# Full-row score matmuls in place of 64-row pairs, and projections issued between retention steps, in a kernel of three blocks

## The chip, the cores and the metric

The kernel runs on one core of a Trainium2 chip. The time is the device time of one execution in microseconds, the median of three runs. A profile is one more execution, taken by the hardware profiler; all rows in this document come from such profiles.

## What is computed

Three blocks follow each other, for 8 batches of 576 positions and 512 channels:

```python
scores = scale * np.matmul(q, k.transpose(0, 1, 3, 2))        # 8 heads of 64
ret = scores * Dmat[None, :, :, :]                            # causal, gamma ** (i - j)
x = np.matmul(ret, v)                                         # retention
...
for e in range(E):                                            # 4 experts of 64
    q = x @ wq[e]; k = x @ wk[e]; v = x @ wv[e]
    scores = np.where(causal, -1000000000.0, scale * (q @ k.transpose(0, 2, 1)))
    a = softmax(scores)
    out += gate_e * (a @ v @ wo[e])                           # top 2 of 4 experts
...
theta = x @ w_theta
y = w_tok_r @ (x * cos(theta)) + w_tok_i @ (x * sin(theta))
u = x + y
out = u + np.maximum(u @ w_ch, 0.0)
```

## The kernel before, in words

**Numbers.** Products that need more precision than one pass gives are made from a high and a low part of each operand: `split` writes the high part on ScalarE and the difference on VectorE, and `mm3` issues three matmuls (high by high, high by low, low by high).

**Stages.** The first half of the span handles retention and the experts' attention, batch by batch; the second half (`z_tile`, `mix`, `channel`) mixes over positions and channels. The change is in the first half.

**Retention** (`ret_fill`) goes over a batch in five chunks of 128 rows (the last has 64). Step c issues the scores of chunk c (`ret_scores`, L125, masked on VectorE at L130 and L133) and the output of chunk c-1 (`ret_out`: state L146, products L153 and L157). The output becomes rows of x: xt on VectorE (L164), its high part xh on ScalarE (L166), its low part xl on POOL (L167). Then the loads of a later chunk are issued on SP's queue, and v is scaled on POOL (L111).

**Projections** read x: `proj_v` for one chunk of rows (12 matmuls of 260 columns), `proj_qk` for half the rows (g) of K (t = 1) or Q (t = 0) of a pair p of experts (12 matmuls of 288 columns). Q goes into `U` [128, 2, S]: for expert s of the pair, one half of the partitions holds the high part and the other half the low part. The high part of K goes into `KN`, and after its second half four DMAs copy it into `KK`, expert by expert, to both halves of the partitions. The low part goes into `KL`.

**Attention** runs in units (batch, pair, row tile m of 5), 80 in all. `at_scores` multiplies for each expert s of the pair all 128 rows of U with KK (high and low of Q times high of K, L272), and then the 64 rows with the high part of Q with KL (L275); VectorE masks the result and takes the minimum (L278), ScalarE makes exp and its sum (L283). `at_norm` scales P (L292 to L299). `at_trans` transposes P on TensorE (L324) and copies it to PT on VectorE for s = 0 and ScalarE for s = 1 (L329, L331). `at_out` multiplies PT with V (L343). It runs when a group of row tiles, (0), (1, 2) or (3, 4), is complete.

**Order.** The loop over units interleaves a unit with *filler*: the second pair's projections of this batch, then everything that the next batch needs first. Each filler has a planned cost; `fill(lim, k)` issues fillers until the planned costs reach `lim`. A unit's planned cost stands in `COST`. A scheduler underneath moves instructions of one engine by the times that it expects itself, so that the built order differs from the written one in places.

**Buffers.** PSUM has four buffers "a" for scores, transposes and value products, and three "w" for retention and projections. `KN` has one buffer, `U`, `KK` and `KL` two.

Of the kernel before, what the change touches and what calls it, by code (L numbers as in the profile page):

```python
# [44 lines left out]
FO = 0.5  # L45
# [8 lines left out]
def tile_kernel(ctx: ExitStack, tc: tile.TileContext, qk, kv, w1, wo, wot, wd, cst, out):  # L54
# [129 lines left out]
    def proj_qk(b, p, t, g):  # L184
        xh, xl = XT[b]
        if (b, p) not in QKP:
            QKP[b, p] = (att.tile([128, 2, S], F32R, name="U", bufs=2), att.tile([128, 2, S], F32R, name="KK", bufs=2),
                         att.tile([128, S], F32R, name="KL", bufs=2), att.tile([128, S], F32R, name="KN", bufs=1))
        U, KK, KL, KN = QKP[b, p]
# [5 lines left out]
        if t:  # L195
            split(KN[:, sl], KL[:, sl], ps)
            if g:
                for s in range(2):
                    for o in range(2):
                        nc.sync.dma_start(KK[o * 64:o * 64 + 64, s, :].bitcast(F32),  # L200
                                          KN[s * 64:s * 64 + 64, :].bitcast(F32))
            return
# [53 lines left out]


    PB, PTB, OB = {}, {}, {}

    def at_scores(u):  # L260
        b, p, m = u
        U, KK, KL, _ = QKP[b, p]
# [6 lines left out]
        for i, (j0, j1) in enumerate(parts):  # L269
            ps = [ps1.tile([128, j1 - j0], F32, name="a", bufs=AB, padded_shape=[128, 512]) for _ in range(2)]  # L270
            for s in range(2):
                nc.tensor.matmul(ps[s][:R], U[:, s, rs], KK[:, s, j0:j1], start=True, stop=False)  # L272
            for s in range(2):
                hs = slice(s * 64, s * 64 + 64)
                nc.tensor.matmul(ps[s][:R], U[hs, s, rs], KL[hs, j0:j1], start=False, stop=True)  # L275
            o = 512 - C * m
            for s in range(2):
                MARK["dve"] = nc.vector.tensor_tensor_reduce(  # L278
                    Ps[s][:R, j0:j1], ps[s][:R], cm[:R, o + j0:o + j1], 1.0, st[:R, 0, s:s + 1] if i else 3.0e38,
                    OP.add, OP.min, st[:R, i, s:s + 1])  # L280
# [231 lines left out]
    COST = [0.7, 1.1, 1.6, 2.2, 2.2]  # L512
    fillers = []
    for b in range(B):
        f1 = qk_fill(b, 1)
        f2 = ret_fill(b + 1) + v_fill(b + 1) + qk_fill(b + 1, 0) if b + 1 < B else []
# [18 lines left out]
    for t in range(nu + 1):  # L535
# [5 lines left out]
        if t < nu:  # L541
            at_scores(units[t])
            done += COST[units[t][2]]
        if t >= 1:
            at_trans(units[t - 1])
        goal = tot * (k + 1) / 10 if t < nu else 1e9
        fill(goal - FO, k)
# [4 lines left out]
        if t < nu:  # L552
            at_norm(units[t])
        fill(goal, k)
# [236 lines left out]
```

## Time and profile before

| | |
|---|---|
| median of 3 runs | 989.08 us (987.85 to 990.68) |
| profiled execution | 989.46 us, span 987.7 us |
| TensorE busy (PE) | 958.8 us, 97% of the span, 8090 matmuls |
| VectorE (DVE) | 683.4 us, 69% |
| ScalarE (ACT) | 487.1 us, 49% |
| GpSimd (POOL) | 226.7 us, 23% |
| granted TensorE clock | 0.991 of full on average |

PE is TensorE's matmuls, PEld its weight loads; the two overlap. Matmul records overlap too, because a matmul's record lasts until its last column has left the array; how fast TensorE goes is read from the starts of the records. L272 is line 272 of the kernel. A timeline merges equal instructions that follow each other into one row with a count. "Idle" is time in which an engine did nothing before an instruction, and behind an arrow stands what ended it; "issue" means that the profile shows nothing that it waited for.

### The profile page before, as it was taken

To read this page: it belongs to the slowest core of one execution; us is meant where nothing else is said; L and a number is where in the kernel's file an instruction comes from. 1 tells how busy PE (TensorE), PEld (TensorE's weight loads), DVE (VectorE), ACT (ScalarE), POOL (GpSimd) and SP (SyncE) were. 2 spreads that over 40 slices of the span, in tenths; PEclk is the share of its full clock that TensorE was granted. 3 is DMA by queue.
4 is the path that set the end of the run, shared out by engine and by line. 5 is a ranking of instruction groups with operands and counts; after the bars stand their busy time and mean duration, and the time that the engine had idled before them with its cause. 6 is when DMAs were issued, how large, how long until landed. Compare 5 with 4: busy or idle time off the path is not lost.

```text
span 987.7 us, 21586 instructions
## 1 busy us (share of the span) xinstructions
PE 958.8 (97%) x8090; PEld 848.1 (86%) x8090; DVE 683.4 (69%) x2099; ACT 487.1 (49%) x1278; POOL 226.7 (23%) x278
## 2 busy tenths in 40 slices
PE   6999999999999999999999999999999999999998
PEld 6988878778787877777767899999999999999998
DVE  5498887888978779687576783485655746486533
ACT  2366656656666565566567652344333432344320
POOL 4334262452624525332000001020200102020110
PEclk9999999999999999999999999999999999999999
DMA  9755563654635636354631301010001001010001
GB/s 267 199 166 155 154 194 89 195 172 124 212 111 171 194 106 204 98 163 132 243 127 37 121 2 48 14 60 25 36 13 37 37 1 49 1 38 12 25 26 48
DMA packets 64185, 101.45 MB, mean 103 GB/s; under 512 B 15184, under 2 KB 37072, under 8 KB 64080
## 3 DMA queue, kind: packets, MB, share of 16 engines
q1 hardware_dynamic: 63936, 99.79, 33.1%
q8 instruction: 64, 1.05, 0.4%
q0 software_dynamic: 144, 0.28, 0.1%
q14 instruction: 41, 0.34, 0.1%
HBM read 67.22 MB, written 23.66 MB: 92 GB/s over the span
## 4 chain that ended last, share of the span: by engine, by line
PE 83%; DVE 10%; DMA 3%; issue 1%; ACT 1%; SPq 1%; POOL 1%; ACTq 0%; POOLq 0%
PE acc L658 24%; PE w L87 12%; PE w L88 11%; PE w L89 11%; PE a L343 4%; PE a L324 4%; PE a L272 3%; PE a L275 2%; PE w L125 2%; PE w L157 2%; PE w L153 2%; PE acc L648 2%; DMA kv<-kv 2%; DVE P L278 2%; DVE sm L130 1%
## 5 line engine op out<-in xcount | busy, mean ns | idle before, releaser
L658 PE MATMUL acc<-TK,zh 128*128 128x256 f32 (+1 forms) x1024 | 183.8, 302 | 0.0
L658 PEld LDWEIGHTS acc<-TK,zh 128*128 128x128 f32 x1024 | 152.4, 190 | 0.7 <-DVE ul L93 0.2
L684 POOL TENSOR_TENSOR o<-o,ul 128x576 f32<-128x576 f32 x28 | 41.9, 1500 | 435.2 <-DVE o L679 435.2
L283 ACT ACTIVATE P<-P,st 128x128 f32<-128x128 f32 (+4 forms) x160 | 95.8, 599 | 69.4 <-DVE st L278 68.6
L658 PE MATMUL acc<-TK,zl 128*128 128x256 f32 (+1 forms) x512 | 110.0, 297 | 0.0
L278 DVE CUSTOM_DVE_ANT_0 P<-a,cm 128x128 f32<-128x128 f32 (+4 forms) x160 | 72.8, 476 | 26.9 <-PE a L275 26.4
L658 PEld LDWEIGHTS acc<-TK,zl 128*128 128x128 f32 x512 | 86.2, 189 | 0.1
L602 ACT ACTIVATE cs<-cs 128x512 f32<-128x512 f32 x72 | 45.2, 630 | 80.3 <-DVE cs L600 76.7
L92 ACT ACTIVATE zh<-cs 128x512 fp32r<-128x512 f32 x64 | 40.2, 630 | 81.3 <-PE acc L658 67.0
L87 PE MATMUL w<-xh,WH 128*128 128x288 f32 x256 | 79.9, 312 | 0.0
L93 DVE TENSOR_TENSOR zl<-cs,zh 128x512 fp32r<-128x512 f32 x64 | 45.0, 707 | 50.4 <-ACT zh L92 49.4
L88 PE MATMUL w<-xl,WH 128*128 128x288 f32 x256 | 76.3, 298 | 0.0
L324 PE MATMUL a<-ident,P 128*128 128x128 f32 (+2 forms) x480 | 65.2, 265 | 11.1 <-DVE P L297 5.2
L87 PE MATMUL w<-uh,CH 128*128 128x256 f32 (+1 forms) x256 | 75.8, 296 | 0.0
L89 PE MATMUL w<-uh,CH 128*128 128x256 f32 (+1 forms) x256 | 75.8, 296 | 0.0
L88 PE MATMUL w<-ul,CH 128*128 128x256 f32 (+1 forms) x256 | 75.8, 296 | 0.0
L89 PE MATMUL w<-xh,WL 128*128 128x288 f32 x256 | 75.6, 295 | 0.0
L604 DVE SCALAR_TENSOR_TENSOR cs<-cs,x 128x512 f32<-128x512 f32 x72 | 55.4, 775 | 24.6 <-ACT cs L602 24.5
L125 PE MATMUL w<-qz,kt 128*64 128x256 f32 (+1 forms) x576 | 61.8, 334 | 7.7 <-DMA kt<-qk 5.1
L167 POOL TENSOR_TENSOR xl<-xt,xh 128x512 fp32r<-128x512 f32 (+1 forms) x40 | 50.7, 1269 | 78.8 <-ACT xh L166 78.8
L324 PEld LDWEIGHTS a<-ident,P 128*128 128x128 f32 (+2 forms) x480 | 45.7, 138 | 26.1 <-DVE P L297 7.4
L93 DVE TENSOR_TENSOR ul<-acc,uh 128x256 fp32r<-128x256 f32 x64 | 25.7, 450 | 59.3 <-ACT uh L92 59.1
(141 smaller groups left out, 2484.7 us busy)
## 6 DMA issues: line engine op xcount, KB each, us to landing
kv<-kv SPq DMA_DIRECT2D x40, 512.0 KB, 4.8
KK<-KN SPq DMA_DIRECT2D x64, 144.0 KB, 2.5
raw<-wd SPq DMA_DIRECT2D x43, 192.0 KB, 2.8
qz<-qk SPq DMA_DIRECT2D x64, 128.0 KB, 4.1
kt<-qk SPq DMA_DIRECT2D x32, 256.0 KB, 3.7
out<-o SPq DMA_DIRECT2D x28, 288.0 KB, 2.1
td<-hl SPq DMA_DIRECT2D x27, 192.0 KB, 2.5
TK<-td SPq DMA_DIRECT2D x9, 576.0 KB, 8.0
```

What stands on the lines that cost most here:

```text
L87: nc.tensor.matmul(ps, ah, bh, start=first, stop=False)
L88: nc.tensor.matmul(ps, ah, bl, start=False, stop=False)
L89: nc.tensor.matmul(ps, al, bh, start=False, stop=last)
L93: nc.vector.tensor_sub(l, src, h)
L125: nc.tensor.matmul(ps[e][g, i, :, j * 64:R], t[:, hp, j * 64:j * 64 + 64], qz[:, :, hp, j * 64:R], start=True, stop=True, skip_group_check ...
L167: nc.gpsimd.tensor_sub(xl[:, :, cs], xt, xh[:, :, cs])
L278: MARK["dve"] = nc.vector.tensor_tensor_reduce(Ps[s][:R, j0:j1], ps[s][:R], cm[:R, o + j0:o + j1], 1.0, st[:R, 0, s:s + 1] if i else 3.0e3 ...
L283: MARK["act"] = nc.scalar.activation(Ps[s][:R, :n], Ps[s][:R, :n], AF.Exp, bias=st[:R, last, s:s + 1], scale=-1.0, accum_out=st[:R, 2, s:s ...
L324: nc.tensor.transpose(tp[:w, j, :], Ps[s][:R, j * C:j * C + w], ident[:R, :R])
L602: nc.scalar.activation(cs, cs, AF.Sin)
L604: nc.vector.scalar_tensor_tensor(z, cs, -1.0, x2[:, None, ds].to_broadcast([128, 2, 256]), op0=OP.mult, op1=OP.mult)
L658: nc.tensor.matmul(acc[d][j], A[:, dc], TK[:, kt, W, t0:t1], start=q == 0 and n == 0, stop=q == 8 and n == 2)
```

## The change

It does four things. The low part of K goes into the same tile as the high part (`KN` and `KK` get one more dimension, `KL` goes), so that the DMAs copy both to both halves of the partitions; `at_scores` then issues for each expert two matmuls with all 128 rows, so that the low part of Q times the low part of K is now computed too. `next_fill` puts V, K and Q projections of the next batch between its retention steps, each after the step that writes the rows that it reads, where they all stood behind the last step before. The unit's order changes: scores, 45% of the filler, normalising of this unit, transposes of the unit before, the rest of the filler, value product. And the planned costs of units are a little larger.

```diff
--- before.py
+++ after.py
@@ -42,7 +42,7 @@
 WARM = 50
 AB = 4
 WB = 3
-FO = 0.5
+FO = 0.45
 NDVE = (0,)
 JR = 82
 EARLY = 9
@@ -184,21 +184,21 @@
     def proj_qk(b, p, t, g):
         xh, xl = XT[b]
         if (b, p) not in QKP:
-            QKP[b, p] = (att.tile([128, 2, S], F32R, name="U", bufs=2), att.tile([128, 2, S], F32R, name="KK", bufs=2),
-                         att.tile([128, S], F32R, name="KL", bufs=2), att.tile([128, S], F32R, name="KN", bufs=1))
-        U, KK, KL, KN = QKP[b, p]
+            QKP[b, p] = (att.tile([128, 2, S], F32R, name="U", bufs=2), att.tile([128, 2, 2, S], F32R, name="KK", bufs=2),
+                         att.tile([128, 2, S], F32R, name="KN", bufs=1))
+        U, KK, KN = QKP[b, p]
         w0 = (2 * p + t) * 128
         sl = slice(g * HS, g * HS + HS)
         ps = ps1.tile([128, HS], F32, name="w", bufs=WB, padded_shape=[128, 512])
         for kt in range(4):
             mm3(ps, WH[:, kt, w0:w0 + 128], WL[:, kt, w0:w0 + 128], xh[:, kt, sl], xl[:, kt, sl], kt == 0, kt == 3)
         if t:
-            split(KN[:, sl], KL[:, sl], ps)
+            split(KN[:, 0, sl], KN[:, 1, sl], ps)
             if g:
                 for s in range(2):
                     for o in range(2):
-                        nc.sync.dma_start(KK[o * 64:o * 64 + 64, s, :].bitcast(F32),
-                                          KN[s * 64:s * 64 + 64, :].bitcast(F32))
+                        nc.sync.dma_start(KK[o * 64:o * 64 + 64, s, :, :].bitcast(F32),
+                                          KN[s * 64:s * 64 + 64, :, :].bitcast(F32))
             return
         for s in range(2):
             i, o = slice(s * 64, s * 64 + 64), slice(64 - s * 64, 128 - s * 64)
@@ -254,12 +254,17 @@
     def v_fill(b):
         return [(1.31, lambda c=c: proj_v(b, c)) for c in range(NCH)] + [(0.0, lambda: gate(b))]
 
+    def next_fill(b):
+
+        r, v, q = ret_fill(b), v_fill(b), qk_fill(b, 0)
+        return [*r[:3], v[0], r[3], v[1], q[0], r[4], v[2], q[2], r[5], v[3], q[1], v[4], v[5], q[3]]
+
 
     PB, PTB, OB = {}, {}, {}
 
     def at_scores(u):
         b, p, m = u
-        U, KK, KL, _ = QKP[b, p]
+        U, KK, _ = QKP[b, p]
         R = ROWS[m]
         n = min(C * (m + 1), S)
         rs = slice(m * C, m * C + R)
@@ -269,10 +274,8 @@
         for i, (j0, j1) in enumerate(parts):
             ps = [ps1.tile([128, j1 - j0], F32, name="a", bufs=AB, padded_shape=[128, 512]) for _ in range(2)]
             for s in range(2):
-                nc.tensor.matmul(ps[s][:R], U[:, s, rs], KK[:, s, j0:j1], start=True, stop=False)
-            for s in range(2):
-                hs = slice(s * 64, s * 64 + 64)
-                nc.tensor.matmul(ps[s][:R], U[hs, s, rs], KL[hs, j0:j1], start=False, stop=True)
+                for x in range(2):
+                    nc.tensor.matmul(ps[s][:R], U[:, s, rs], KK[:, s, x, j0:j1], start=x == 0, stop=x == 1)
             o = 512 - C * m
             for s in range(2):
                 MARK["dve"] = nc.vector.tensor_tensor_reduce(
@@ -509,11 +512,11 @@
         X2[g, i], NR[g, i] = x2, nr
 
     units = [(b, p, m) for b in range(B) for p in range(2) for m in range(NCH)]
-    COST = [0.7, 1.1, 1.6, 2.2, 2.2]
+    COST = [0.9, 1.2, 1.7, 2.2, 2.4]
     fillers = []
     for b in range(B):
         f1 = qk_fill(b, 1)
-        f2 = ret_fill(b + 1) + v_fill(b + 1) + qk_fill(b + 1, 0) if b + 1 < B else []
+        f2 = next_fill(b + 1) if b + 1 < B else []
         fillers.append(f1 + f2)
 
     nu = len(units)
@@ -541,17 +544,17 @@
         if t < nu:
             at_scores(units[t])
             done += COST[units[t][2]]
+        goal = tot * (k + 1) / 10 if t < nu else 1e9
+        fill(done + FO * max(goal - done, 0.0), k)
+        if t < nu:
+            at_norm(units[t])
         if t >= 1:
             at_trans(units[t - 1])
-        goal = tot * (k + 1) / 10 if t < nu else 1e9
-        fill(goal - FO, k)
+        fill(goal, k)
         if t >= 1:
             ub, up, um = units[t - 1]
             if GROUPS[GRP[um]][-1] == um:
                 at_out(ub, up, GRP[um])
-        if t < nu:
-            at_norm(units[t])
-        fill(goal, k)
 
 
         for _ in range(0 if t < 2 else t * JR // 100 - (t - 1) * JR // 100):
```

Behind the change, lines of the kernel are 3 to 6 higher: the scores are L278, the mask L281, exp L286, the normalising L295 to L302, the transposes L327, the copies L332 and L334, the value product L346.

How the built order changes shows at three places, all in the middle of the first half. First on TensorE, scores of row tile 2 while projections are the filler (L272 and L275, after L278: scores; L324, after L327: transposes; L343, after L346: value product; L87 to L89: the three matmuls of a projection, of V where `WH` stands before `xh`, of K or Q the other way round). Before:

```order
L87 MATMUL w<-WH,xh 128x260
L88 MATMUL w<-WL,xh 128x260
L89 MATMUL w<-WH,xl 128x260
L272 MATMUL a<-KK,U 128x384 x2
L275 MATMUL a<-KL,U 128x384 x2
L324 MATMUL a<-ident,P 128x128 x4
L87 MATMUL w<-WH,xh 128x260
```

After:

```order
L89 MATMUL w<-WH,xl 128x260
L346 MATMUL a<-PT,V 64x128 x2
L278 MATMUL a<-KK,U 128x384 x4
L87 MATMUL w<-xh,WH 128x288
L88 MATMUL w<-xl,WH 128x288
L89 MATMUL w<-xh,WL 128x288
...
L89 MATMUL w<-xh,WL 128x288
L327 MATMUL a<-ident,P 128x128 x4
L153 MATMUL w<-qz_110,S_107 64x64 x8
```

The 64-row pair is gone, four equal matmuls stand in its place, and a whole projection stands between them and the transposes.

Second on TensorE, a retention step that ends with L157, and scores of row tile 0. Before:

```order
L272 MATMUL a<-KK,U 128x128 x2
L275 MATMUL a<-KL,U 128x128 x2
L125 MATMUL w<-qz_110,kt 64x2x64 x3
L324 MATMUL a<-ident,P 128x64 x4
L324 MATMUL a<-ident,P 64x64
...
L125 MATMUL w<-qz_110,kt 64x2x64
L146 MATMUL pS<-vp,kv 64x64 x8
L153 MATMUL w<-qz_109,S_108 64x128 x8
L157 MATMUL w<-sm_114,vp 64x128 x2
...
L157 MATMUL w<-sm_115,vp 64x128 x2
L343 MATMUL a<-PT,V 64x192 x8
```

After:

```order
L157 MATMUL w<-sm_113,vp 64x128 x2
L278 MATMUL a<-KK,U 128x128 x4
L87 MATMUL w<-WH,xh 128x260
L88 MATMUL w<-WL,xh 128x260
L89 MATMUL w<-WH,xl 128x260
...
L327 MATMUL a<-ident,P 128x64 x4
L327 MATMUL a<-ident,P 64x64
...
L87 MATMUL w<-xh,WH 128x288
L88 MATMUL w<-xl,WH 128x288
L89 MATMUL w<-xh,WL 128x288
...
L346 MATMUL a<-PT,V 64x192 x8
```

Before, the next retention step (L125, L146, L153, L157) stood around the transposes of row tile 4 and ahead of their value product (L343). Now a V projection stands ahead of the transposes, and a K projection, which reads the rows of x that this retention step makes, behind them and ahead of the value product.

Third on ScalarE, in the same stretch: xh is the copy that makes rows of x, V, KN and U are the results of the V, K and Q projections. Before:

```order
L166 ACTIVATE xh<-xt 128x4x128
...
L166 ACTIVATE xh<-xt 128x4x64
...
L226 COPY V<-w 128x256
...
L92 ACTIVATE KN<-w 128x288
...
L205 ACTIVATE U<-w 64x288 x2
```

After:

```order
L166 ACTIVATE xh<-xt 128x4x128
...
L226 COPY V<-w 128x256
...
L92 ACTIVATE KN<-w 128x288
...
L166 ACTIVATE xh<-xt 128x4x128
L226 COPY V<-w 128x256
...
L205 ACTIVATE U<-w 64x288 x2
...
L166 ACTIVATE xh<-xt 128x4x64
...
L226 COPY V<-w 128x256
...
L92 ACTIVATE KN<-w 128x288
```

Before, all copies to xh of a batch stood ahead of all projections; now the projections stand between them.

## Rows read from the trace of the kernel before

**Rows 1.** Stretches of core 0: length; PE, PEld, DVE, ACT, POOL busy; PEclk; DMA.

```profile
237.40:298.60 61.20, 60.71 (x618) 50.02 (x619) 50.63 (x190) 38.95 (x118) 26.92 (x36) 1.00 0.56 164
302.90:330.20 27.30, 26.35 (x317) 20.72 (x318) 25.47 (x85) 16.65 (x46) 14.89 (x18) 0.94 0.66 197
330.20:363.20 33.00, 31.80 (x268) 27.49 (x265) 23.57 (x98) 20.88 (x67) 13.41 (x19) 1.00 0.41 119
```

**Rows 2.** Timeline of TensorE: start us, us, engine, line, operation, out<-in, shapes, count.

```profile
300.25 0.50 PE L272 MATMUL a<-KK,U 128*128 128x256 f32 x2
300.69 0.38 PE L275 MATMUL a<-KL,U 64*128 64x256 f32 x2
301.00 0.44 PE L324 MATMUL a<-ident,P 128*128 128x128 f32 x2
...
301.41 0.29 PE L88 MATMUL w<-xl,WH 128*128 128x288 f32 x1
301.54 0.29 PE L89 MATMUL w<-xh,WL 128*128 128x288 f32 x1
...
304.63 0.62 PE L272 MATMUL a<-KK,U 128*128 128x384 f32 x2
...
305.55 0.66 PE L324 MATMUL a<-ident,P 128*128 128x128 f32 x4
...
308.93 0.73 PE L272 MATMUL a<-KK,U 128*128 128x512 f32 x2
...
310.02 1.52 PE L125 MATMUL w<-qz,kt 128*64 128x256 f32 x16
...
315.82 0.48 PE L272 MATMUL a<-KK,U 128*64 128x288 f32 x2
...
316.51 0.48 PE L272 MATMUL a<-KK,U 128*64 128x288 f32 x2
...
322.75 0.44 PE L272 MATMUL a<-KK,U 128*128 128x128 f32 x2
...
323.38 0.66 PE L125 MATMUL w<-qz,kt 128*64 128x128 f32 x8
```

**Rows 3.** Waits of TensorE and its weight loads: us in total, times, longest us.

```profile
PE a L324 <- DVE P L297: 5.2, 7, 1.4
...
PE a L324 <- DVE st L278: 2.9, 4, 1.3
PE a L324 <- ACT ob L347: 2.8, 2, 1.5
...
PE a L272 <- DMA KK<-KN: 0.3, 1, 0.3
...
PEld a L275 <- issue: 16.4, 63, 0.4
```

**Rows 4.** Lower-clock stretches, first and last of 4; columns as in rows 1.

```profile
138.60:142.00 3.40, 3.40 (x42) 3.40 (x40) 2.62 (x11) 1.65 (x6) 2.15 (x3) 0.50 0.87 266
...
398.00:401.40 3.40, 3.40 (x38) 3.06 (x39) 1.25 (x5) 1.48 (x6) 2.61 (x3) 0.50 0.40 136
```

**Rows 5.** Timeline of all engines: transposes of one unit and their last copy.

```profile
311.58 0.87 PE L324 MATMUL a<-ident,P 128*128 128x128 f32 x6
...
314.40 0.24 ACT L331 COPY PT<-a 128x128 f32<-128x128 f32 x1
```

**Rows 6.** Timeline of all engines: from the retention output to xl.

```profile
322.86 0.69 DVE L164 TENSOR_TENSOR xt<-w,gt 128x512 f32<-128x512 f32 x1 [0.27 <-PE w L157]
...
323.39 1.04 POOL L111 TENSOR_TENSOR vp<-kv,gam 128x512 f32<-128x512 f32 x1 [0.42 <-DMA kv<-kv]
...
324.40 1.88 POOL L167 TENSOR_TENSOR xl<-xt,xh 128x512 fp32r<-128x512 f32 x1
```

**Rows 7.** DMA issues: out<-in, engine, operation, count, KB each, us to landing.

```profile
KK<-KN SPq DMA_DIRECT2D x64, 144.0 KB, 2.5
...
od<-ob SPq DMA_DIRECT2D x16, 288.0 KB, 2.7
```

## The prediction

> **What bounds the kernel now.** I read the busy time by stretches first. One batch of the first half, the one with the fewest waits, takes 61.2 us: TensorE is busy for 60.7 of them, VectorE for 50.6, ScalarE for 39.0 [rows 1]. So TensorE's order of instructions sets the time there, with VectorE close behind. The two parts of a batch differ: while retention steps follow each other VectorE is busy for 25.5 of 27.3 us (93%), and while projections follow each other for 23.6 of 33.0 us (71%) [rows 1]. The second half of the kernel (mixing and channels) is not touched by the change, and I leave it as it is.
>
> TensorE's busy share hides its losses, because a matmul's record covers its whole passage. I therefore read the timeline by starts: from the first matmul of a group to the start of what follows. A score group of 256 columns takes from 300.25 to 301.00, 0.75 us [rows 2]. It holds two full-row matmuls and two of 64 rows, and the two of 64 rows run side by side (together 0.38 us, [rows 2]). Back-to-back full-row matmuls of 288 columns start 0.13 us apart (301.41, 301.54, [rows 2]): 0.120 us of columns at the 2.4 GHz level and 0.013 us more. So 0.75 us is spent where the columns of one pair after another would need 3 x 0.12 = 0.36. The rest is lost where the shape of the array changes: before the 64-row pair the weight loads stood still for 16.4 us in all, 63 times, with no releaser, up to 0.4 us each [rows 3].
>
> Last the waits. TensorE waited for a releaser most in front of the transposes: 5.2 + 2.9 + 2.8 = 10.9 us [rows 3]. Soon after such waits the granted clock fell to the lower level, 1.2 GHz, in four stretches of 3.4 us; the first and the last stand in [rows 4].
>
> **The change, part by part.**
>
> *Scores with full rows.* The 64-row pair is replaced by two full-row matmuls, and KL is doubled up inside KK. TensorE's number of matmuls stays the same. Now, per unit, from the first score matmul to the start of what follows: 0.63 us at 128 columns (322.75 to 323.38), 0.75 at 256, 0.92 at 384 (304.63 to 305.55), 1.09 at 512 (308.93 to 310.02) and twice 0.69 for the last tile's halves (315.82 to 316.51) [rows 2]: 4.77 us per pair of experts and batch, 76.3 us for the 16 of them. After: four full-row matmuls in a row at their spacing. At 288 columns that is 0.133; by the same 0.013 us on top of the columns it is 0.12 at 256, 0.173 at 384 and 0.227 at 512; at 128 columns I take the spacing of the transposes, 0.105 (six take 0.87 us and four 0.66, [rows 2, 5]). Four times these, and eight times 0.133 for the last tile, is 3.56 us. One entry from a column-tiled product stays per unit. The 256-column pair took 0.44 us until the 64-row pair began, against 0.24 for its two spacings: 0.20 for entry and exit together [rows 2]; I take 0.1 for an entry, 0.5 for five: 4.06 us, 65.0 for all. In the built order 21 of the 80 units are followed by a retention step, which still costs an exit, 0.1 each: 2.1. So 76.3 - 67.1 = 9.2 us, and a little more, since what follows the other 59 units (transposes or projections, full rows too) no longer has to load its first weights in the open. I take **-10**, with ends of -6 (half the exits cost more than 0.1) and -14.
>
> *A rule against this.* The rows show the 64-row pair sharing the array, 0.38 us for both [rows 2]. The Trainium skill ("TensorE: Matmul & The Clock Gate", Part 3: Packing small matmuls) says that matmuls of few rows, placed in different row groups, run concurrently and that packing them so is the gain. The trace agrees on the concurrency; what the change of shape costs, the page doesn't say there. By the rule alone the sum would have a plus of some 14 us in place of -10 (worked out under the rivals).
>
> *Transposes later, normalising earlier.* The transposes of unit t-1 move behind the scores of unit t and about 45% of its filler, and the normalising of unit t is issued before them. What a transpose waits for (P scaled by VectorE or ScalarE) is then a unit old. The 10.9 us go; ends 0 and -10.9. The four stretches at half clock (13.6 us, in which half the time is lost) cost up to 6.8 us. I count them as following those waits: **-10.9** and **-6.8**; ends 0 for the clock too.
>
> What is late next is the copy of the transposed tile. Now the value product stands behind nearly all filler; after, it stands behind the rest, 12 projection matmuls (12 x 0.13 = 1.6 us) or at the last tile 7 to 12 (0.9 to 1.6). In one unit now the transposes start at 311.58, the last copy ends at 314.40 + 0.24 = 314.64, 2.2 us after the last transpose, since the masks of the unit just scored stand ahead of the copies on VectorE [rows 5]. After, those masks lie a filler earlier. I take 0.15 us for each of some 32 value products with the short cover: **+5**, ends 0 and 32 x 0.6 = 19.
>
> *Projections between retention steps.* The same instructions in another order. In the pure retention stretch VectorE was at 93% [rows 1]; with projections between the steps it has time to catch up, which is what lets the waits above go. The risk is the chain that makes rows of x: mask on VectorE, copy on ScalarE, difference on POOL. From 322.86 (xt starts) to 324.40 + 1.88 (xl ends) it took 3.42 us [rows 6]. By the built order the first K projection of a batch stands behind four score matmuls (0.5), a V projection (12 x 0.12 = 1.5), ten small transposes (between half and all of 10 x 0.105; I take 0.7) and one matmul of its own (0.13) after the product that yields its last rows: 2.8 us of cover, 0.6 short. Seven batches at 0.6 to 0.8: **+5**. Ends: 0, if POOL is free, and 7 x 1.6 = 11, if one scaling of v (1.04 us, [rows 6]) stands ahead on POOL. Every projection after it has longer cover in the order.
>
> *K copies of twice the size.* KK<-KN moves 144 KB in 2.5 us now; the copy of 288 KB out of ob needs 2.7 [rows 7]. Between the second K projection and the first scores that read it the built order has a value product, scores, a V and a Q projection, eight transposes and part of the next K projection, some 6 us (the 24 projection matmuls of V and Q alone are 3.1). Four copies issue one after another on SP within that. I cost this at **0**; without the cover it would be up to 0.5 us for each of 8 batches, 4 us. KN is written again only in the second half of that stretch, so its single buffer costs nothing either. A gain is excluded: TensorE waited for these copies 0.3 us in all [rows 3].
>
> Sum: -10 - 10.9 - 6.8 + 5 + 5 = -17.7. From the profiled execution's 989.46 us that is 971.8; the median of the runs, 989.08, is 0.04% lower, so I leave it at **972**.
>
> **The rivals.**
>
> *Row packing was worth its switches (slower).* If the lost time around the 64-row pair were not due to the change of shape, it would stay, and the second KL matmul would be added to each unit: 16 x (0.105 + 0.12 + 0.173 + 0.227 + 2 x 0.133) = 14 us: **1004**. It decides where the entry and exit cost less than the added matmul, 0.12 us at 256 columns; against it the rows show 0.39 us there [rows 2]. 4%.
>
> *New waits take the place of the old (slower).* The chain to x and the tile copies are longer than their cover on a loaded VectorE, and the clock goes on falling. The gains are 27.7 us in all, 4 us in each of seven batches; with 3 us at the K projection and 2 us over the value products per batch (+35), and no clock gained back, it is -10 - 10.9 + 35 = +14: **1003**. It speaks against it that the short covers miss by 0.6 us in the rows I found. 6%.
>
> *VectorE becomes the bound.* It needs 50.6 us a batch [rows 1], and the aim is about 59. If its in-order queue leaves half of the waits, only the scores' part and a few us more are left: -4 to -12, about **981**. 20%.
>
> *Nothing measurable.* Saved scores go into waits: within 3 us of now, 8%.
>
> *Nothing new is waited for.* -10 - 10.9 - 6.8, and the stalls of the retention stretch besides: **961** or less, 12%.
>
> **How the numbers follow.** My forecast (-12 to -26) has 50%. The range reaches from 960, at the edge of the case without new waits, to 988, which leaves out the two slow rivals and part of "nothing measurable". About 0.3%, 3 us, is what a measurement of this kernel can tell from no change: faster 0.50 + 0.20 + 0.12 and a little of the fourth case = 0.83; same 0.08; slower 0.09.
>
> **What would show it.** Right: the groups of score matmuls take 0.54, 0.59, 0.8, 1.0 and 1.1 us by starts; the pause in front of a 64-row pair is gone; transposes wait under 3 us in all; at most one or two stretches at half clock. Wrong: score groups as long as now or longer; waits of value products on PT copies, or of the first K projection on xl, above 1 us in each batch; waits on KK<-KN; VectorE above 90% over whole batches.

## The result and the profile after

The changed kernel takes 1001.87 us (median of 4 runs, 1000.29 to 1004.67) against 988.47 for the kernel before in 4 runs beside it: ratio 1.0142, 95% interval 1.0101 to 1.0182. It is slower by 13 us, outside the range of the prediction, on the side to which 0.09 was given. Every ratio below is against the kernel before in runs beside it (their medians lie between 985.0 and 988.5 us), so I compare changed kernels with each other by their ratios.

I begin with the waits of TensorE and its weight loads (us in total, times, longest), which answer to [rows 3]:

```profile
PE w L125 <- DMA kt<-qk: 9.0, 3, 3.6
PE w L88 <- POOL xl L167: 7.0, 7, 2.7
PE a L346 <- DVE PT L332: 4.3, 7, 1.0
PE a L278 <- DMA KK<-KN: 4.3, 4, 1.4
PE a L346 <- DVE PT L334: 2.4, 3, 0.9
...
PE a L346 <- ACT PT L334: 0.9, 1, 0.9
...
PE a L327 <- DVE st L281: 0.8, 2, 0.6
...
PEld a L278 <- issue: 5.8, 33, 0.3
```

The transposes' waits are nearly gone (0.8 us in place of 10.9), and the pause of the weight loads ahead of scores fell from 16.4 to 5.8 us. In their place stand waits on xl (7.0), on tile copies (7.6 in these three rows) and on the copies of K (4.3, where it was 0.3). (The row at the head, on kt, belongs to the start-up; there it was 5.1 before.) The timeline of TensorE answers to [rows 2]:

```profile
305.04 0.33 PE L278 MATMUL a<-KK,U 128*128 128x128 f32 x2
305.30 0.82 PE L327 MATMUL a<-ident,P 64*128 64x64 f32 x10
...
308.89 0.74 PE L278 MATMUL a<-KK,U 128*128 128x256 f32 x4
309.46 0.30 PE L87 MATMUL w<-xh,WH 128*128 128x288 f32 x1
...
313.73 0.98 PE L278 MATMUL a<-KK,U 128*128 128x384 f32 x4
314.64 0.43 PE L125 MATMUL w<-qz,kt 128*64 128x256 f32 x1
...
318.52 1.17 PE L278 MATMUL a<-KK,U 128*128 128x512 f32 x4
319.61 0.65 PE L125 MATMUL w<-qz,kt 128*64 128x256 f32 x4
```

By starts a group takes 0.57 us at 256 columns, 0.91 at 384 with an exit into a retention step, 1.09 at 512; two matmuls at 128 columns take 0.26, which makes 0.52 for four. At 128 and 256 columns the scores do what was forecast (0.54 and 0.59); the groups shown at 384 and 512 end with an exit into a retention step and take as long as those in [rows 2] did. The DMA issues (count, KB each, us to landing) answer to [rows 7]:

```profile
KK<-KN SPq DMA_DIRECT2D x64, 288.0 KB, 4.9
...
od<-ob SPq DMA_DIRECT2D x16, 288.0 KB, 4.2
```

A K copy now lands after 4.9 us (the median), where 2.5 was measured before. The lower clock answers to [rows 4]; after the start-up, six stretches of 3.4 us are at the lower level, where four were: four in the first seven batches, as before, and two in the last batch, which had none. This row covers most of the first:

```profile
84.00:87.40 3.40, 3.40 (x21) 2.78 (x21) 2.85 (x12) 1.44 (x4) 1.64 (x4) 0.53 0.28 65
```

**Where the time went.** I cut each profiled execution where TensorE starts the first scores of a batch, and where it starts to mix; "mixing" ends with TensorE's last matmul, some 4 us ahead of the span's end (us, from the timelines; each row is one execution):

| profile | up to the first scores | batches 1 to 7 | last batch | mixing | span |
|---|---|---|---|---|---|
| before | 46.0 | 438.7 | 69.1 | 429.9 | 987.7 |
| changed | 50.6 | 440.1 | 75.5 | 429.8 | 1000.4 |
| e5_kzero | 45.6 | 440.5 | 68.8 | 430.0 | 989.0 |
| e8_fo20 | 48.1 | 433.6 | 75.5 | 430.2 | 991.4 |
| e12_copies | 47.8 | 450.1 | 69.7 | 429.9 | 1001.7 |
| e13_traffic | 47.9 | 437.2 | 70.6 | 430.0 | 989.7 |
| e10_kzero_fo20_late | 45.1 | 422.3 | 68.9 | 429.9 | 970.2 |

Of the change's 12.7 us, 4.6 lie ahead of the first scores, 6.4 in the last batch, 1.4 in the seven batches. Inside those seven, counted by starts (from one matmul to the next, so that a wait is charged to what stands ahead of it), scores fell by 6.6 us, transposes by 5.8, retention by 12.3. But K and Q projections rose by 17.0, though 16 fewer of their matmuls lie in this part, V projections by 3.5 and value products by 5.6. The gain was real and was spent again. The trace shows on what, if the seven batches are split into TensorE's waits (its idle times over 0.15 us), what the clock took (half of the time at the lower level, at most) and the rest, in which matmuls follow each other:

| batches 1 to 7 | us | waits | clock | rest |
|---|---|---|---|---|
| before | 438.7 | 11.4 | 6.8 | 420.5 |
| changed | 440.1 | 22.8 | 6.8 | 410.5 |
| e5_kzero | 440.5 | 22.7 | 8.5 | 409.2 |
| e11_scores_kzero | 432.2 | 17.9 | 1.7 | 412.6 |
| e12_copies | 450.1 | 18.7 | 5.1 | 426.3 |
| e13_traffic | 437.2 | 12.9 | 3.4 | 420.9 |
| e10_kzero_fo20_late | 422.3 | 10.9 | 0.0 | 411.3 |

The change made the rest 10.0 us shorter, but the waits doubled.

At the first batch little is there to cover a longer copy: in the built order 17 more projection matmuls (2.3 us) stand ahead of the first scores. Another 1.7 of the 4.6 us are clock: at the start 6.8 us lie at the lower level, where 3.4 did; e6 and e8, with the same copies and 3.4 us there, reach the first scores after 48.2 and 48.1. Later the copies look like this (SyncE's queue and TensorE):

```profile
362.47 3.51 SPq L200 DMA_DIRECT2D KK<-KN  x4
...
367.59 0.41 PE L278 MATMUL a<-KK,U 128*128 128x128 f32 x2 [1.13 <-DMA KK<-KN]
...
510.42 0.33 SPq L461 DMA_DIRECT2D th<-tt  x1
510.80 1.10 SPq L200 DMA_DIRECT2D KK<-KN  x2
516.99 0.33 SPq L461 DMA_DIRECT2D th<-tt  x1
...
521.29 0.77 PE L87 MATMUL a<-th,wt 128*128 128x512 f32 x1 [1.68 <-DMA th<-tt]
```

Four issues keep SyncE for 3.5 us, and the scores start 5.1 us after the first, 1.13 of it in a plain wait. In the last batch two of the four copies are issued behind a load of th, 11.8 us after the first two (1.8 before); ahead of the two loads shown SyncE waited 8.2 us for the product on TensorE that still read the one buffer of th (5.7 before). TensorE's waits in the last batch are 6.6 us against 4.1, none of them on a copy of K, and the two stretches at the lower level take 3.4: together 5.9 of the 6.4 us. How much of that is due to the copies is open: in single executions the last batch takes 67.3 to 72.9 us in the kernels with short copies and 67.6 to 75.5 in those with long ones.

### The profile page after: what moved, and what is told of

It reads as the page before. It is cut to its first block, busy times and chain, and to the rows that moved or that the text cites. A ratio compares the mean times of both kernels' runs of the same rounds, so it can differ in the third digit from the quotient of the medians.

```text
span 1000.4 us, 21540 instructions
## 1 busy us (share of the span) xinstructions
PE 955.3 (95%) x8090; PEld 858.2 (86%) x8090; DVE 685.4 (69%) x2099; ACT 486.8 (49%) x1278; POOL 226.0 (23%) x278
## 4 chain that ended last, share of the span: by engine, by line
PE 72%; DVE 14%; DMA 6%; ACT 3%; issue 2%; POOL 1%; SPq 0%; ACTq 0%; POOLq 0%; DVEq 0%
PE acc L661 23%; PE w L89 10%; PE w L88 10%; PE w L87 10%; PE a L278 4%; PE a L346 4%; PE w L125 3%; DVE P L281 3%; PE a L327 3%; PE acc L651 2%; DMA KK<-KN 2%; PE w L157 2%; DVE P L300 2%; PE w L153 1%; DVE sm L130 1%
## 5 line engine op out<-in xcount | busy, mean ns | idle before, releaser
L286 ACT ACTIVATE P<-P,st 128x128 f32<-128x128 f32 (+4 forms) x160 | 95.8, 599 | 72.9 <-DVE st L281 72.3
L281 DVE CUSTOM_DVE_ANT_0 P<-a,cm 128x128 f32<-128x128 f32 (+4 forms) x160 | 72.8, 477 | 37.9 <-PE a L278 37.1
L278 PE MATMUL a<-KK,U 128*64 128x288 f32 (+4 forms) x384 | 80.0, 330 | 8.5 <-DMA KK<-KN 4.3
L88 PE MATMUL w<-xl,WH 128*128 128x288 f32 x256 | 78.5, 307 | 7.0 <-POOL xl L167 7.0
L605 ACT ACTIVATE cs<-cs 128x512 f32<-128x512 f32 x72 | 45.1, 629 | 80.3 <-DVE cs L603 76.4
L87 PE MATMUL w<-xh,WH 128*128 128x288 f32 x256 | 78.9, 308 | 0.2 <-ACT xh L166 0.2
L89 PE MATMUL w<-xh,WL 128*128 128x288 f32 x256 | 77.9, 304 | 0.0
L87 PE MATMUL w<-uh,CH 128*128 128x256 f32 (+1 forms) x256 | 75.8, 296 | 0.0
L89 PE MATMUL w<-uh,CH 128*128 128x256 f32 (+1 forms) x256 | 75.8, 296 | 0.0
L278 PEld LDWEIGHTS a<-KK,U 128*128 128x128 f32 (+1 forms) x384 | 55.1, 172 | 22.2 <-issue 5.8
L346 PE MATMUL a<-PT,V 128*64 128x192 f32 (+3 forms) x576 | 64.0, 330 | 8.7 <-DVE PT L332 4.3
L125 PE MATMUL w<-qz,kt 128*64 128x128 f32 (+1 forms) x576 | 60.4, 333 | 9.4 <-DMA kt<-qk 9.0
L346 PEld LDWEIGHTS a<-PT,V 128*64 128x64 f32 (+1 forms) x576 | 38.7, 138 | 32.7 <-DVE PT L332 6.9
```

The lines of the kernel that those rows point to most:

```text
L87: nc.tensor.matmul(ps, ah, bh, start=first, stop=False)
L88: nc.tensor.matmul(ps, ah, bl, start=False, stop=False)
L89: nc.tensor.matmul(ps, al, bh, start=False, stop=last)
L125: nc.tensor.matmul(ps[e][g, i, :, j * 64:R], t[:, hp, j * 64:j * 64 + 64], qz[:, :, hp, j * 64:R], start=True, stop=True, skip_group_check ...
L278: nc.tensor.matmul(ps[s][:R], U[:, s, rs], KK[:, s, x, j0:j1], start=x == 0, stop=x == 1)
L281: MARK["dve"] = nc.vector.tensor_tensor_reduce(Ps[s][:R, j0:j1], ps[s][:R], cm[:R, o + j0:o + j1], 1.0, st[:R, 0, s:s + 1] if i else 3.0e3 ...
```

## The experiments

**Each part alone.** e1_scores puts the full-row scores with their doubled copies into the kernel before, e2_order the unit's new order, e3_fill the projections between the retention steps. e4_no_fill is the changed kernel without the last.

```diff
 e1_scores (before; with KN, KK as in the change)
-  U[:, s, rs] x KK[:, s]   and   U[hs, s, rs] x KL[hs]
+  U[:, s, rs] x KK[:, s, 0]   and   U[:, s, rs] x KK[:, s, 1]
 e2_order (before; FO 0.45)
-  scores(t); trans(t-1); fill; out(t-1); norm(t); fill
+  scores(t); 45% of fill; norm(t); trans(t-1); fill; out(t-1)
 e3_fill (before)
-  f2 = ret_fill(b + 1) + v_fill(b + 1) + qk_fill(b + 1, 0)
+  f2 = next_fill(b + 1)
 e4_no_fill (changed)
-  f2 = next_fill(b + 1)
+  f2 = ret_fill(b + 1) + v_fill(b + 1) + qk_fill(b + 1, 0)
```

> The kernel before with the full-row scores (and the doubled K copies) alone, old unit order, old filler order, old planned costs. Theory A (the score groups got cheaper as forecast and the loss is in the new order): the score groups give 6 to 8 us, the wait on the doubled K copies takes back 2 to 5 us, so 0 to -6 us against before, about 985. Rival B (sharing the array by 64-row pairs was worth its switches): +10 to +14 us, about 1001.

> The kernel before with the new unit order alone (normalising and transposes behind 45% of the filler). Theory A: the waits of transposes on scaled P (10.9 us) go to under 3, the value products wait 5 to 8 us on tile copies instead, so -6 to +1 us against before. Rival C (the new order is itself what costs): the value products' waits are larger than what the transposes gave, +5 us or more.

> The kernel before with the projections between the retention steps alone. Theory A: the first K projection of seven batches waits for xl, 7 to 10 us in all with the lower clock behind it, little is won elsewhere: +4 to +10 us against before. Rival D (VectorE is relieved and that outweighs it): the waits before transposes fall by half and the time is 2 to 6 us below before.

> The changed kernel with the old filler order (all retention steps, then V, then K and Q): full-row scores and new unit order stay. Theory A: without the waits on xl it is 8 to 14 us faster than the changed kernel, 988 to 994. Rival D: the retention steps crowd VectorE again and it is as slow as the changed kernel or slower, 1000 or more.

Measured: e1 997.16 us, ratio 1.0112 [1.0053, 1.0172]; e2 1006.33, 1.0193 [1.0137, 1.0250]; e3 987.01, 1.0006 [0.9984, 1.0027]; e4 992.70, 1.0070 [1.0043, 1.0097]. No part alone gains, and two lose; for e1 and e2 my theory had allowed +1 us at most. The parts don't add up either: 11 + 19 + 1 would be 31 us. Without the projections between the retention steps the changed kernel is 7 us faster (e4, by the two ratios). The wait that e2's order makes stands at the head of its waits:

```profile
PE a L343 <- DVE PT L329: 17.3, 10, 2.9
```

The value products, now close behind their transposes, wait for the tile copies. e1's loss fitted "the 64-row pair was worth its place", but also "the doubled copies cost". The next group separates these.

**The copies.** e5_kzero is the changed kernel with copies of 144 KB: VectorE writes the low part of K straight into a tile with a half of zeros. With it the product of the two low parts, which the change had added, is left out again; the number of matmuls and their shapes stay. e11_scores_kzero puts such scores into the kernel before. e12_copies leaves the scores of before alone and only doubles the copies, with zeros that nobody reads.

```diff
 e5_kzero (changed), e11_scores_kzero (before): copies of KN [128, S]
+  nc.vector.tensor_sub(KLZ[(2 * b + p) % 2][hs, s, sl], ps[hs], KN[hs, sl])
-  KK[:, s, x, j0:j1] for x in range(2)
+  KX[:, s, j0:j1] for KX in (KK, KLZ[(2 * b + p) % 2])
 e12_copies (before): KN2[:, 1] is zero
-  dma_start(KK[o * 64:o * 64 + 64, s, :], KN[s * 64:s * 64 + 64, :])
+  dma_start(KK[o * 64:o * 64 + 64, s, :, :], KN2[s * 64:s * 64 + 64, :, :])
```

> The changed kernel with the low part of K written by VectorE straight into a tile whose other half stays zero, so that the copies move 144 KB again (the product of the two low parts is left out, as in the kernel before). Theory A (the doubled copies land too late): landing back to about 2.5 us, the wait on KK<-KN and the gaps between projections and first scores go, 5 to 8 us faster than the changed kernel, about 995. Rival E (the copies are covered elsewhere and VectorE decides): VectorE gets 32 instructions of 0.45 us more, and the time is the same or up to 6 us longer.

> The kernel before with the full-row scores alone, but with copies of 144 KB (low part of K in place, zero half). Theory A (the scores alone were slow by 11 us because of the doubled copies): at or below before, -6 to 0 us. Rival G (a faster score group only turns into waits on VectorE and ScalarE): +4 us or more again, waits of transposes on scaled P at 10 us or above.

> The kernel before with its K copies doubled to 288 KB and nothing else (the added half is zeros that nobody reads). Theory A: landing near 4.9 us, +5 to +12 us against before, a good part of it after the first half's last batch has begun. Rival G: within 3 us of before.

Measured: e5 989.43, 1.0040 [1.0021, 1.0058]; e11 982.16, 0.9950 [0.9928, 0.9972]; e12 1004.46, 1.0179 [1.0149, 1.0209]. So the doubled copies, with the order that is built for them, cost the kernel before 18 us, and taking them out of the changed kernel gives 10 us back by the two ratios (11 between the two profiles). The two prices lie at different places. In the changed kernel it is the two ends: 5.0 us ahead of the first scores and 6.7 in the last batch, clock included, and nothing in the seven batches. In e12 it is the seven batches, 11.4 of the 14 us between the profiles, and the ends give 2.4. The full-row scores themselves are worth 0.5%, some 5 us, in the old order; the 64-row pair was not worth its switches.

In e12 TensorE hardly waits for a copy, though. Its waits:

```profile
PE a L324 <- DVE P L297: 11.7, 13, 2.0
PE a L324 <- ACT ob L347: 3.4, 3, 1.5
...
PE a L343 <- DVE PT L329: 1.7, 3, 0.7
...
PE a L272 <- DMA KK<-kn: 0.6, 2, 0.4
```

**How the copies cost.** Four ways were open: the traffic (e13_traffic adds the same bytes in copies that nobody waits for), a batch's first scores standing later (e14_late_first), ScalarE's wait to overwrite the K tile (e15_copies_kn2), and a split: the order built for e12 puts the second expert's first scores 23 projection matmuls behind the first's (e16_split makes the split alone, e17_copies_late takes it out of e12).

```diff
 e13_traffic (before)
+  KD = att.tile([128, 2, S], F32, name="KD", bufs=2)
+  dma_start(KD[o * 64:o * 64 + 64, s, :], ZS[s * 64:s * 64 + 64, :])   # x4
 e14_late_first (before), e17_copies_late (e12): at k == 0, ahead of at_scores
+  two fillers of F
 e15_copies_kn2 (e12)
-  KN2
+  KN2[p]
 e16_split (before): at k == 0, between the scores of s = 0 and s = 1
+  two fillers of F
```

> The kernel before, with four more copies behind each head pair's K copies: 64 partitions x 2304 bytes from a tile of zeros into a tile that nobody reads. Bytes moved and issues on SyncE's queue are at least those of e12_copies, but no instruction waits for the added copies, and TensorE's order stays that of before. Theory T (the traffic itself, or SyncE's issues and the loads behind them, cost the 18 us of e12): slower by 10 us or more. Theory L (the copies cost by the time at which the scores can start, that is by the place that the built order gives them): within 4 us of before.

> The kernel before, with 144 KB copies, and the first unit's scores of each batch written behind the first two K projections of the next head pair: they stand 20 projection matmuls (2.7 us by starts) later on TensorE, as the scores of the second expert do in e12_copies (23). No transfer is added. Theory L: slower by 8 us or more, though TensorE waits for no copy there (K copies under 0.5 us of waits), with the lost time in waits behind the scores: transposes on VectorE's P, value products on tile copies, lower clock. Theory T: within 3 us of before.

> e12_copies (K copies of 288 KB, half of them zeros that nobody reads) with two K tiles in turn, so that ScalarE no longer waits to overwrite a K tile that the copies still read; TensorE's order is that of e12. Theory N (ScalarE's wait of 2.1 us for that tile, and what queues behind it, costs much): half or more of e12's +18 us goes, to +9 or less. Theory L and theory T: +13 to +19 still.

> The kernel before, with 144 KB copies and no transfer added; of each batch's first unit the second expert's scores are written behind the first two K projections of the next head pair, the first expert's stay where they are. So a first unit's scores stand in two pieces, 20 projection matmuls apart, as in the order built for e12_copies (23) and for the changed kernel (24). Theory P (the split is what costs: the first expert's probabilities are ready early, the second's late, and the masks, exponentials and transposes of the next units crowd behind them): slower by 8 us or more. Theory Q (the split costs nothing; the longer copies cost by where they lie beside other transfers, or by the rest of the built order): within 4 us of before, as e14, where both pieces stand late, was.

> e12_copies (K copies of 288 KB) with the first unit's scores written behind two projections of the next head pair, as in e14: the two pieces now stand 4 to 9 matmuls apart instead of 23, and 45 projection matmuls (some 6 us) cover a landing of 4.6 us. Theory P: most of e12's +18 us goes, to +5 or less. Theory Q: +12 or more stays.

Measured: e13 990.45, 1.0037 [1.0014, 1.0061]; e14 982.28, 0.9966 [0.9942, 0.9990]; e15 1012.26, 1.0265 [1.0210, 1.0320]; e16 987.71, 1.0013 [0.9990, 1.0035]; e17 1001.90, 1.0161 [1.0116, 1.0207]. The traffic is worth 4 of the 18 us; later scores gain a little; the split, my theory by then, falls twice. On ScalarE's wait e15 says only that nothing was won: its built order is not that of e12, and one wait of 8.4 us near the end of the first half is of another kind.

What is left shows in VectorE's timeline at the last row tile. In the kernel before the normalising of P (L297, 512 columns) ran ahead of the last tile's four masks (L278):

```profile
317.05 0.48 DVE L297 TENSOR_SCALAR P<-P,st 128x512 f32<-128x512 f32 x1
...
317.71 0.44 DVE L278 CUSTOM_DVE_ANT_0 P<-a,cm 64x288 f32<-64x288 f32 x1
```

In e12 it runs behind three of them and takes 1.34 us in place of 0.48, for which no run shows a reason; the transposes wait for it:

```profile
327.80 0.44 DVE L278 CUSTOM_DVE_ANT_0 P<-a,cm 64x288 f32<-64x288 f32 x1
...
328.25 0.43 DVE L278 CUSTOM_DVE_ANT_0 P<-a,cm 64x288 f32<-64x288 f32 x1
...
329.32 0.50 DVE L278 CUSTOM_DVE_ANT_0 P<-a,cm,st 64x288 f32<-64x288 f32 x1
...
329.76 1.34 DVE L297 TENSOR_SCALAR P<-P,st 128x512 f32<-128x512 f32 x1
...
331.15 1.09 PE L324 MATMUL a<-ident,P 128*128 128x128 f32 x8 [1.00 <-DVE P L297]
```

Nothing in the source moved them. The scheduler underneath orders by the times that it expects, and with longer copies it weaves each engine's instructions otherwise. Counted over the 80 units of the built order, 10 masks of a next unit stand ahead of a normalising in the kernel before; 10 in e13, 11 in e14, 10 in e16, 10 in e11, none more than 4 us slower; 29 in e12, 25 in e17, 19 in e15, 37 in e1, all 11 to 26 us slower. But these last four all have long copies in the old order of units, as has e7 below (20 masks, 20 us slower), so the count doesn't tell the built order from the copies; nor does it rank them, since e1 has most masks and lost least. The seven batches of e12 are 11.4 us longer than those of the kernel before: its waits are 7.3 us longer, the clock took 1.7 less, and 5.8 lie in the rest, where the trace shows no wait of TensorE. Over the whole span the waits of transposes on P grew by 6.5 (11.7 against 5.2), those on the copies by 0.3, and the bytes cost 4 where the order stayed (e13). That the moved masks are the cause is argued, not shown: no run has the long copies in the old built order.

**The covers.** e6_k_later gives the first K projection its missing cover; e7_old_unit takes the unit's new order out of the changed kernel; e8_fo20 issues 20% of the filler ahead of the transposes in place of 45%. e9 and e10 put these on e5.

```diff
 e6_k_later (changed); also in e10 and e18
-  r[3], v[1], q[0], r[4], v[2]
+  r[3], v[1], r[4], q[0], v[2]
 e7_old_unit (changed): unit's order and FO of before
 e8_fo20 (changed); also in e9, e10 and e18
-FO = 0.45
+FO = 0.2
 e9_kzero_fo20 = e5 + FO 0.2;  e10_kzero_fo20_late = e9 + the order of e6
 e18_after_late = e8 + the order of e6 + the late first scores of e14
```

> The changed kernel with the first K projection of a batch one retention step later, behind the step after the one that makes its last rows. Theory A (it waits for xl): waits on xl from 7.0 us to under 1.5, 5 to 9 us faster than the changed kernel. Rival F (the wait only moves: the value product of the last row tile loses its cover, 0.5 us instead of 1.6): value products wait 4 us or more longer and the time is within 3 us of the changed kernel.

> The changed kernel with the old unit order (transposes straight behind the next scores, normalising late). Theory A: waits on tile copies fall from 8 us to under 3, waits of transposes on scaled P come back to 7 to 12, the time is within 5 us of the changed kernel. Rival C (the new unit order is what costs): 8 us or more faster than the changed kernel.

> The changed kernel with the transposes behind 20% of the unit's filler instead of 45%. Theory A (value products stand too close behind the tile copies): waits on tile copies from 8 us to under 4, waits of transposes below 3, 3 to 7 us faster than the changed kernel. Rival C: no change in the time, since the copies are late because VectorE is.

> The changed kernel with both single mends: the low part of K in place with a zero half (copies of 144 KB) and the transposes behind 20% of the filler. If the two costs are separate, their gains add: 12 us and 8 us off the changed kernel, about 982, 3 us below before. If both mends remove the same waits, it stays near the better of the two, 987 to 991.

> The same with the first K projection one retention step later. Theory A (with 20% the value product of the last row tile keeps a V projection as cover, so that the wait on xl no longer moves there): waits on xl under 1.5 us and on tile copies under 4 us, 3 to 6 us below the kernel without this, about 978. Rival F (VectorE, on which xl and the copies both wait, decides): same as the kernel without it within 2 us.

> The changed kernel with its doubled copies and the whole product, with three changes of order alone: FO 0.2, the first K projection one retention step later (as e10), and the first unit's scores written behind two projections of the next head pair (as e14). Theory P: the pieces stand 1 to 5 matmuls apart, and the time is near e10's, -6 to -14 us against the kernel before. Theory Q: it stays with e8 (994) or above before.

Measured: e6 1003.81, 1.0197 [1.0158, 1.0236]; e7 1005.10, 1.0214 [1.0173, 1.0254]; e8 993.95, 1.0090 [1.0062, 1.0118]; e9 987.49, 1.0015 [0.9991, 1.0039]; e10 **975.27**, 0.9880 [0.9859, 0.9902]; e18 997.88, 1.0105 [1.0048, 1.0161].

e7 is 0.7% slower than the changed kernel, so the unit's new order is not what costs there. e6 took the waits on xl away, and they came back as waits on tile copies, since the K projection had been the value product's cover:

```profile
PE a L346 <- DVE PT L332: 14.1, 11, 3.9
...
PE a L278 <- DMA KK<-KN: 3.7, 4, 1.4
```

e8 shows that 0.45 was too much: with the larger share of filler behind the transposes the waits on tile copies fall to 0.9 us. Its seven batches are 6.5 us shorter, 4.7 of it waits; the last batch stays as long as it was, and the first scores come 2.5 us earlier. The two mends don't add: e9 has both and is 0.25% under e5. In e10 no wait of the seven batches is over 1.6 us, and together they are 10.9 us, where the kernel before had 11.4 (the rows are of the whole span; the longest, on kt, is in the start-up):

```profile
PE w L125 <- DMA kt<-qk: 6.6, 4, 2.5
PE a L330 <- DVE st L284: 4.9, 9, 1.5
...
PE a L281 <- ACT ob L353: 1.6, 1, 1.6
PE a L330 <- DVE P L303: 1.5, 1, 1.5
...
PE a L349 <- ACT PT L335: 1.3, 4, 0.4
```

and a stretch of 60 us in the middle (length; PE, PEld, DVE, ACT, POOL busy; PEclk) runs almost without a gap (0.23 us) at the full clock:

```profile
210.00:270.00 60.00, 59.77 (x628) 52.55 (x627) 53.23 (x201) 39.94 (x123) 25.12 (x34) 1.00 0.57 172
```

It is 1.2% faster than the kernel before (11 to 12 us), with the same three products for the scores, and by the two ratios 2.6% faster than the changed kernel. e18 tried the same with the doubled copies kept, and the first scores later, and failed.

## Why the prediction was wrong, step by step

*K copies of twice the size* is the step that failed: "I cost this at 0", with at most 4 us. With the order built for them they cost 10 (e5 against the changed kernel) to 18 (e12). The step set the 2.7 us of ob, one copy that goes out alone to DRAM, against some 6 us of cover. But four K copies follow one another, and the long ones land one behind the other: the last lands 8.0 us after the first is issued (the median of 16 groups), where it was 4.5. The 6 us cover the first expert's two copies alone (4.9 us); the second expert's scores, which stood 0 to 3 projection matmuls behind the first's in batches 2 to 8, stand 23 or 24 behind them in the new built order. And the step looked at the middle of the run alone. It did not look at the two ends: ahead of the first scores (+4.6, of which 1.7 are clock), where 2.3 us could be read in the built order, and the last batch (+6.4, of which 3.4 are clock), where the copies share SyncE's queue with the loads of th. Neither had a term in my sum. Last, the step read one built order, but did not ask what another landing time does to it: in e12 TensorE waits 0.6 us for copies, and the kernel loses 18. Which part of that is the order is open.

*Scores with full rows*: right. Forecast -10; by starts the scores fell by 6.6 us in seven batches and by 2.3 in the last, 8.9 in all; in e11, in the old order, the whole kernel gained some 5, since its waits grew. *A rule against this* did not decide: by the rule of the Trainium skill ("TensorE: Matmul & The Clock Gate", Part 3: Packing small matmuls) the four full-row matmuls should have cost more than the packed pair. In the groups of the timeline they cost less at 128 and 256 columns (0.52 against 0.63 us, 0.57 against 0.75) and as much at 384 and 512.

*Transposes later, normalising earlier*: its first term was right, 10.1 of the 10.9 us of waits went; but TensorE's waits as a whole doubled in the seven batches, so they moved rather than went. The term for the clock is the second step that failed. Forecast was -6.8; the seven batches have four stretches at the lower level as before, and with the last batch and the start-up the clock took 5 us more, not less. I had bounded the term at 0, as if no new wait could make new stretches. It was too large besides, since I read it off one execution: in 83 runs of the kernel before that stand beside the experiments the granted clock was 0.994 on average (986.3 us), not the 0.991 of my profile, and the 23 with 0.997 or more took 983.6, so some 3 us were to be had. The +5 for the value products was mis-sized when the order stands alone (17.3 us of waits in e2); in the changed kernel, with projections between the steps, they were 7.6.

*Projections between retention steps*: right in mechanism and nearly in size, 7 waits on xl, 7.0 us, against +5, and 7 us less without these projections (e4). But the price of repairing it was not seen: the K projection that comes too early is also the cover of the value product (e6). Only with FO at 0.2 is there cover for both (e10, 12 us under e9).

Of the rivals, *new waits take the place of the old* is the one that came, and its time, 1003, is 1 us from the result, but by luck: it needed 35 us at the K projection and the value products, where 14.6 were seen, and it missed the copies. I gave it 6% because each cover that I looked at missed by 0.6 us only. *Row packing was worth its switches* would have given 1004 and is excluded by e11. Taking the copies and the two covers out, e10's span is 17.5 us under that of before, where the sum said 17.7; that is luck too. Its profile is the fastest of its six runs, and by the medians e10 gains 11. In the profiles the seven batches give 9.2 us in the rest and 6.8 by the clock, and only 0.5 in waits, so of the sum the term of the scores came true, and the waits as a whole hardly fell.

## What to carry to other kernels

Price a group of larger transfers from the first issue to the last landing, by a row of the same kind of copy, and look for it where nothing covers it: at the first and the last turn of a loop and on the queue that it shares. If a scheduler builds the order, one changed duration can move instructions on every engine, so read the new order on the engine next to the bound (here masks slid ahead of the normalising), before a cost is put at nothing. Before a clock term goes into a sum, look at the clock of several executions: one profile is one draw. A cover can be spent only once: before an instruction is moved to hide one wait, ask which wait it was hiding.

## What the runs showed of the hardware

Copies that follow one another queue. Landing times of the K copies before and in the changed kernel (tile KK), and the rows of e13 (its copies of zeros and its K copies) and e12:

```profile
DMA to landing us min/median/max: 2.2/2.5/4.2
...
DMA to landing us min/median/max: 3.0/4.9/7.7
...
KD<-zs SPq DMA_DIRECT2D x64, 144.0 KB, 2.9
...
KK<-KN SPq DMA_DIRECT2D x64, 144.0 KB, 2.5
...
KK<-kn SPq DMA_DIRECT2D x64, 288.0 KB, 4.6
```

By their place among the four, the copies of 144 KB land after 2.3, 2.5, 2.6 and 2.6 us (medians), those of 288 KB in the changed kernel after 3.2, 4.2, 5.3 and 5.9. So the first long copy takes 0.9 us more, and the fourth 3.3. Between the first issue and the last landing a packet takes 165 ns at 2304 bytes and 349 ns at 4608 (medians in most groups), about as its bytes. I estimate from this, with the 64 packets of a copy spread evenly over 16 DMA engines, 0.7 and 1.4 us for a copy. They are issued 0.5 to 0.9 us apart, so the short ones keep pace and the long ones fall behind. SyncE needs 3.5 us to issue four of the long ones, where it mostly needed 2.4 to 2.5 before. The 288 KB of ob took 2.7 us [rows 7], but that copy differs in three things (128 partitions, into DRAM, alone), and no run tells them apart.

The clock can make a wait dearer than its length. In the changed kernel the waits on xl stand where lower stretches begin (at 84, 210 and 340 us):

```profile
210.54 0.61 PE L88 MATMUL w<-xl,WH 128*128 128x288 f32 x1 [2.74 <-POOL xl L167]
...
339.46 0.40 PE L88 MATMUL w<-xl,WH 128*128 128x288 f32 x1 [2.03 <-POOL xl L167]
...
340.34 0.45 PE L89 MATMUL w<-xh,WL 128*128 128x288 f32 x1
340.58 0.45 PE L87 MATMUL w<-xh,WH 128*128 128x288 f32 x1
```

Behind the wait of 2.03 us matmuls of 288 columns start 0.24 us apart, at 1.2 GHz by the granted clock, where [rows 2] have 0.13; over 3.4 us that is about 1.5 us lost besides the wait, so I estimate that a wait of 2 us there costs 3.5. Even 0.94 us, at 83.31, was followed by such a stretch. The length of a wait alone doesn't tell, though: in the kernel before a wait of 2.03 us, at 549.3, brought none, while the same one in the changed kernel, at 560.3, did; and in the profiled execution of e10 the clock stayed up in all seven batches, with waits of up to 1.6 us.
